# A planner that lets a freed place rest, and one step's transposed weights put ahead of a later step's scores

## The chip, the cores and the metric

One core of one Trainium2 chip. The time is that of one execution in device microseconds. Before the change three runs gave 855.59, 857.68 and 860.67 us; the median, 857.68 us, is what a run of the changed kernel is set against. TensorE is PE below (its weight loads PEld), VectorE is DVE, ScalarE is ACT, GpSimd is POOL, and SP is the queue that issues every load and store.

## The reference, cut to what matters

Three layers in float32. The first is attention that keeps the 32 largest scores of each row; the second mixes four experts; the third is a gated product.

```python
# batch 2, heads 8, 576 positions, head size 64
scores = q @ k.T / 8
kth    = 32nd largest of each row
attn   = softmax(where(scores >= kth, scores, -1e9)) @ v      # -> x, 1152 x 512
p      = domain_probs / sum(domain_probs)                     # 1152 x 4
x      = sum over e of p[:, e] * (relu(x @ w1[e]) @ w2[e])    # w1 512 x 1024, w2 1024 x 512
out    = ((x @ w_a) * (x @ w_b)) @ w_out                      # d_ff 1536
```

## The kernel before, in words

The 1152 tokens lie in nine tiles of 128; the tiles form groups of 1, 2, 3 and 3 (`GROUPS`). Attention goes in 36 steps, counted from n = 0: for each group, for each of four pairs of heads, for each tile of the group. The first group has one tile, so its four pairs are the first to the fourth step (n = 0 to 3). The text counts steps from one: the fourth step is n = 3, the sixth is n = 5.

A step does, for each of its two heads j: `scores` (eight matmuls of 288 columns for the two heads, and ACT's copy of the result at L613 into a place of `ss`); `masked`, which finds the 32 largest on DVE by four MAX8 (L633) and three MATCH_REPLACE8 (L641) for each head; the exponentials and the mask; and `weigh`, which transposes the weights on PE ("turns" them, five transposes a head at L371), copies the result on ACT (L738, L742) into a place of `pts`, and multiplies by v (20 matmuls that read `low` and `vrem`). After a pair's last tile the result is copied to x; for the first group that is L770, into `xf`. The fourth step (`URGENT = 3`) ends the first group, and so has a shorter form of the mask (`hurried`, L698 on ACT, L704 to L709 on DVE).

The first group's experts (`plain`) can finish their first layer only with all four pairs of `xf`: the matmuls `ps<-xf,raw` add up over the pairs, one eight of matmul records for each; L958 then makes the relu on ACT, and the second layer follows (`ps<-raw,low`). Expert weights come by SP into four places of `raw`, and every fifth into `ys`. The later groups' experts are `experts`, with matmuls in three parts (high by high, high by low, low by high) whose results ACT (L870) and DVE (L874, L892) take out of PSUM. The last layer is `gated`.

PSUM has eight banks, held as three kinds of places: `ms` (three single banks, for the experts), `atts` (two pairs of banks, for scores and for every transposed operand of attention) and `os_` (one bank, for weights by v). Places in SBUF belong to a region; `ss` has four, `pts` three.

The order of all instructions is worked out ahead by `Plan.order()`, which walks a calendar with estimated durations. Whenever an engine is free at a point of the calendar, it takes the ready operation with the smallest key whose places are free. Instructions are then issued on each engine in that fixed order; the chip waits by semaphores. An operation that follows another sees its end `SEEN` = 45 ns later, or `SEEN_PE` = 130 ns later where it runs on PE. A place, however, counts as free in the calendar at the instant at which its last user ends.

Places of one kind are handed out in a fixed order as well: each request has a `need`, requests are sorted by it (`settle`), and `place` gives nothing to a request whose turn has not come. For `atts`, `need` equals the operation's key: n - 2.4 for scores (`AHEAD`), n + 0.5 for a step's turned weights, and n - 0.06 for the fourth step's. So the order on the two pairs of banks around the change is: third step's turned weights (2.5, twice), sixth step's scores (2.6, twice), fourth step's turned weights (2.94, twice), then the keys of the next pair of the second batch (3.02, 3.03) and the queries of a later pair (3.04, twice).

Of the kernel before, what the change touches and what calls it, by code (L numbers as in the profile page):

```python
# [34 lines left out]
class Slots:  # L35


    def __init__(self, name, aps, region=None, spans=None):
        self.name, self.aps, self.region, self.spans = name, aps, region, spans
        self.free = set(range(len(aps)))  # L40
        self.queue, self.next = [], 0

    def tile(self, need=0.0):
        t = Buffer(self, need)
        self.queue.append(t)
        return t
# [25 lines left out]
SEEN, SEEN_PE = 45, 130  # L72
# [3 lines left out]
class Plan:  # L76
# [14 lines left out]
    def order(self):  # L91
        for op in self.ops:
            op.left, op.at = len(op.waits), op.since
            for w in op.waits:
                w.after.append(op)
        late, ready, free, events, tick = {}, {}, {}, [], 0
        for op in self.ops:
            for table, empty in ((late, []), (ready, [])):
                table.setdefault(op.engine, list(empty))
            free.setdefault(op.engine, 0.0)  # L100
        for op in self.ops:
            if not op.left:
                heapq.heappush(late[op.engine], (op.at, op.n, op))
        regions = {}
        for s in {id(t.slots): t.slots for op in self.ops for t in op.tiles}.values():
            s.settle()
        for op in self.ops:
            for t in op.tiles:
                s = t.slots
                if s.region is not None and s not in regions.setdefault(s.region, []):  # L110
                    regions[s.region].append(s)
        dma_free, lanes = 0.0, []
        queue, now, done = [(op.since, -1, None) for op in self.ops if op.since], 0.0, []
        heapq.heapify(queue)
        seq = 0

        def place(t):
            s = t.slots
            if t.slot is not None:
                return t.slot  # L120
            if t.n != s.next:
                return None
            for i in sorted(s.free):
                if s.spans is None:
                    return i
                a0, a1 = s.spans[i]
                for o in regions[s.region]:
                    if o is s or o.done:
                        continue
                    if any(a0 < b1 and b0 < a1 for b0, b1 in o.spans):  # L130
                        if o.rank < s.rank or any(
                            j not in o.free and a0 < o.spans[j][1] and o.spans[j][0] < a1 for j in range(len(o.aps))
                        ):
                            break
                else:
                    return i
            return None

        def pick(engine):
            late_, ready_ = late[engine], ready[engine]  # L140
            while late_ and late_[0][0] <= now:
                _, _, op = heapq.heappop(late_)
                heapq.heappush(ready_, (op.key, op.n, op))
            skipped, found = [], None
            stuck = set()
            while ready_:
                item = heapq.heappop(ready_)
                op = item[2]

                ok = not (op.port and free.get("POOL", 0.0) > now)  # L150
                for t in op.tiles:
                    if t.slot is None and (t.slots in stuck or place(t) is None):
                        stuck.add(t.slots)
                        ok = False
                if ok:
                    found = op
                    break
                skipped.append(item)
                if len(skipped) > 60:
                    break  # L160
            for item in skipped:
                heapq.heappush(ready_, item)
            return found

        while len(done) < len(self.ops):
            moved = False
            for engine in free:
                if free[engine] > now:
                    continue
                if engine == "SP" and len(lanes) >= LANES and lanes[-LANES] > now:  # L170
                    continue
                op = pick(engine)
                if op is None:
                    continue
                moved = True
                for t in op.tiles:
                    if t.slot is None:
                        t.slot = place(t)
                        t.slots.free.discard(t.slot)
                        t.slots.next += 1  # L180
                op.start = now
                done.append(op)
                if engine == "SP":
                    free[engine] = now + ISSUE
                    dma_free = max(dma_free, now + ISSUE) + op.nbytes / GBS
                    end = dma_free + LAND
                    lanes.append(end)
                else:
                    free[engine] = now + op.hold
                    end = now + op.hold + op.lag  # L190
                heapq.heappush(queue, (end, op.n, op))
                heapq.heappush(queue, (free[engine], -1, None))
            if moved:
                continue
            if not queue:
                raise RuntimeError("the plan stands still: " + str([(o.n, o.engine, o.key) for o in self.ops if o.start is None][:8]))
            now = max(now, queue[0][0])
            while queue and queue[0][0] <= now:
                _, _, op = heapq.heappop(queue)
                if op is None:  # L200
                    continue
                for t in op.tiles:
                    t.users -= 1
                    if not t.users:
                        t.slots.free.add(t.slot)
                for a in op.after:
                    a.left -= 1
                    a.at = max(a.at, now + (SEEN_PE if a.engine == "PE" else SEEN))
                    if not a.left:
                        heapq.heappush(late[a.engine], (a.at, a.n, a))  # L210
                        heapq.heappush(queue, (a.at, -1, None))
        self.span = now
        return sorted(self.ops, key=lambda o: (o.start, o.n))
# [27 lines left out]
URGENT = 3  # L241


def body(tc, q, k, v, probs, w1, w2, wa, wb, wo, out):
# [109 lines left out]
    def scalar(n, emit, key, after, tiles, sbuf=False, ptr=False, extra=0):  # L354
        return plan.add("ACT", act(n, sbuf, ptr) + extra, emit, key, after, tiles, lag=110)
# [8 lines left out]
    def tensor(hold, emit, key, after, tiles):  # L364
        return plan.add("PE", hold, emit, key, after, tiles, lag=165)
# [4 lines left out]
    def tr(out, a, i):  # L370
        nc.tensor.transpose(out, a, i)  # L371
# [344 lines left out]
    def weigh(pair, i, ed, n):  # L716

        t, T = pair.tiles[i], pair.T
# [3 lines left out]
        pt, ptd = [], []  # L722
        for e, done in ed:

            kt = n + (-0.06 if n == URGENT else 0.5)
            at, p = atts.tile(kt), pts.tile(n)

            def turn(e=e, at=at):
                a = at.ap.rearrange("p b (m c) -> p (b m) c", c=128)
                for m in range(M4):  # L730
                    tr(a[:, m], e.ap[:, m * 128:(m + 1) * 128], ident)
                tr(a[0:REM, M4], e.ap[:, MAIN:S], ident)

            o = tensor(4 * TURN_F + 80, turn, kt, [done, ready], [at, e])

            def ev0(at=at, p=p):
                a = at.ap.rearrange("p b (m c) -> p (b m) c", c=128)
                nc.scalar.activation(p.ap[:, 0:MAIN].rearrange("p (m c) -> p m c", c=128), a[:, 0:M4], AF.Copy)  # L738

            def ev1(at=at, p=p):  # L740
                a = at.ap.rearrange("p b (m c) -> p (b m) c", c=128)
                nc.scalar.activation(p.ap[0:REM, MAIN:MAIN + 128], a[0:REM, M4], AF.Copy)  # L742

            ke = -3000 if n == URGENT else -900
            ptd.append(scalar(512, ev0, ke, [o], [at, p]))
            ptd.append(scalar(128, ev1, ke, [o], [at, p]))
            pt.append(p)
# [367 lines left out]
```

## Time and profile before

| | |
|---|---|
| runs | 855.59, 857.68, 860.67 us; median 857.68 |
| profiled execution | 854.94 us |
| its span | 853.2 us, 14162 instructions |
| busy: PE, PEld, DVE, ACT, POOL | 818.9, 726.6, 717.9, 539.5, 265.4 us |
| mean granted PE clock | 0.989 of full |

The profile is that of one execution. Its page gives each engine's busy time; a second view gives the same for any stretch of the span, with the granted clock (1.00 is 2.4 GHz, 0.50 is 1.2 GHz) and the mean busy share of the 16 DMA engines. A list by time gives each engine's instructions with the idle time before them and, behind an arrow, what ended it. The list of waits adds such idle times up. Matmul ends are modelled, so a run of matmuls is best timed from its first start to the start of what follows.

### The profile page before, as it was taken

What the parts mean: (1) busy time and instruction counts of PE and PEld (TensorE: products, weight loads), DVE (VectorE), ACT (ScalarE), POOL (GpSimd) and SP (SyncE); (2) the same over time, 40 slices, a digit from 0 to 9 for tenths busy, and PEclk for the clock granted to TensorE, in tenths of its full rate; (3) what the DMA queues carried; (4) which work ended last, traced back from release to release, by engine and by line L of the source; (5) the groups of instructions that cost most, each with busy time, mean ns of one, the idle gap of its engine ahead of it and who ended that gap; (6) DMA issues with size and microseconds to landing.
All of it is one profiled execution on the core that took longest, in us unless ns stands there. A gap on an engine that the chain in (4) does not pass through costs nothing.

```text
span 853.2 us, 14162 instructions
## 1 busy us (share of the span) xinstructions
PE 818.9 (96%) x5168; PEld 726.6 (85%) x5168; DVE 717.9 (84%) x1387; ACT 539.5 (63%) x1034; POOL 265.4 (31%) x250
## 2 busy tenths in 40 slices
PE   6689999999999999999999999999999999999997
PEld 5467777789888989888888788899899989999996
DVE  7999999999999999999969999555435888989723
ACT  6878887979989799887656654333225535344210
POOL 4524443897897965863110000000000000000000
PEclk9699999999999999999999999999999999999999
DMA  5939977754564535232345555333001322323003
GB/s 177 284 113 273 334 229 239 222 171 160 171 206 137 176 122 178 77 123 75 99 124 170 188 186 173 123 124 124 1 1 50 99 72 77 99 80 95 25 1 111
DMA packets 83509, 117.06 MB, mean 137 GB/s; under 512 B 10608, under 2 KB 54640, under 8 KB 83440
## 3 DMA queue, kind: packets, MB, share of 16 engines
q1 hardware_dynamic: 83440, 116.17, 43.5%
q8 instruction: 40, 0.66, 0.3%
q14 instruction: 29, 0.24, 0.1%
HBM read 109.07 MB, written 7.08 MB: 136 GB/s over the span
## 4 chain that ended last, share of the span: by engine, by line
PE 73%; DVE 15%; ACT 5%; issue 3%; POOL 2%; DMA 1%; DVEq 0%; POOLq 0%; ACTq 0%
PE ps L368 68%; PE ps L371 5%; DVE low L633 4%; DVE low L641 4%; DVE mid L800 2%; DVE mid L874 1%; ACT mid L799 1%; ACT low L664 1%; POOL low L668 1%; DVE ys L892 1%; DMA raw<-in_moe_w_dram 1%; POOL big L428 1%; ACT low L613 1%; ACT low L683 1%; ACT low L672 0%
## 5 line engine op out<-in xcount | busy, mean ns | idle before, releaser
L368 PE MATMUL ps<-xs,mid 128*128 128x384 f32 (+1 forms) x1152 | 205.9, 322 | 4.0 <-DVE mid L874 3.0
L633 DVE MAX8 low<-low 128x8 f32<-128x576 f32 x288 | 203.8, 746 | 2.2 <-ACT low L613 2.0
L368 PE MATMUL ps<-mid 128*128 128x512 f32 x768 | 197.1, 396 | 1.6 <-DVE mid L874 1.2
L368 PEld LDWEIGHTS ps<-xs,mid 128*128 128x128 f32 x1152 | 183.9, 188 | 14.7 <-DVE mid L874 4.4
L368 PEld LDWEIGHTS ps<-mid 128*128 128x128 f32 x768 | 139.6, 188 | 30.7 <-DVE mid L874 7.2
L641 DVE MATCH_REPLACE8 low<-low 128x576 f32<-128x576 f32 x216 | 159.2, 742 | 0.0
L368 PE MATMUL ps<-xs,big 128*128 128x384 f32 x864 | 152.8, 335 | 0.0
L368 PEld LDWEIGHTS ps<-xs,big 128*128 128x128 f32 x864 | 149.9, 188 | 1.6 <-DVE low L1066 0.3
L799 ACT ACTIVATE mid<-raw 128x1024 fp32r<-128x1024 f32 x96 | 101.3, 1063 | 76.9 <-PE ps L368 36.7
L800 POOL TENSOR_TENSOR mid<-raw,mid 128x1024 fp32r<-128x1024 f32 x48 | 114.9, 2405 | 4.9 <-ACT mid L799 4.5
L668 POOL TENSOR_TENSOR low<-low 128x576 f32<-128x576 f32 x70 | 98.9, 1427 | 38.8 <-ACT low L664 36.1
L368 PE MATMUL ps<-big,mid 128*128 128x512 f32 x324 | 75.0, 390 | 0.0
L800 DVE TENSOR_TENSOR mid<-raw,mid 128x1024 fp32r<-128x1024 f32 x48 | 59.3, 1236 | 17.1 <-ACT mid L799 17.0
L368 PEld LDWEIGHTS ps<-big,mid 128*128 128x128 f32 x324 | 60.7, 188 | 12.3
L892 DVE SCALAR_TENSOR_TENSOR ys<-ps,pr,ys 128x512 f32<-128x512 f32 x56 | 41.5, 746 | 24.8 <-PE ps L368 24.3
L874 DVE SCALAR_TENSOR_TENSOR mid<-ps,mid 128x384 fp32r<-128x384 f32 (+1 forms) x96 | 48.0, 505 | 13.7 <-ACT mid L870 13.6
L683 ACT ACTIVATE low<-low 128x576 f32<-128x576 f32 x70 | 51.4, 776 | 11.4 <-DVE low L680 11.3
L1045 ACT ACTIVATE low<-ps 128x384 f32<-128x384 f32 x36 | 17.6, 490 | 64.0 <-PE ps L368 64.0
L870 ACT ACTIVATE mid<-ps 128x384 fp32r<-128x384 f32 (+1 forms) x96 | 43.1, 452 | 22.0 <-PE ps L368 15.1
L664 ACT ACTIVATE low<-low 128x576 f32<-128x576 f32 x70 | 52.8, 778 | 4.3 <-POOL low L658 4.2
L672 ACT ACTIVATE low<-low 128x576 f32<-128x576 f32 x70 | 54.5, 779 | 0.7 <-POOL low L668 0.7
L613 ACT ACTIVATE low<-ps 128x576 f32<-128x576 f32 x72 | 46.5, 650 | 12.5 <-PE ps L368 6.6
(87 smaller groups left out, 1042.9 us busy)
## 6 DMA issues: line engine op xcount, KB each, us to landing
raw<-in_moe_w_dram SPq DMA_DIRECT2D x122, 512.0 KB, 3.8
big<-kscr SPq DMA_DIRECT2D x20, 576.0 KB, 5.1
low<-in_v_dram SPq DMA_DIRECT2D x24, 256.0 KB, 3.7
low<-in_moe_w_a_dram SPq DMA_DIRECT2D x12, 512.0 KB, 3.8
low<-in_moe_w_b_dram SPq DMA_DIRECT2D x12, 512.0 KB, 3.8
low<-in_moe_w_out_dram SPq DMA_DIRECT2D x12, 512.0 KB, 3.6
kscr<-big SPq DMA_DIRECT2D x8, 576.0 KB, 5.3
ys<-in_moe_w_dram SPq DMA_DIRECT2D x6, 512.0 KB, 5.8
```

The costliest lines, as they stand in the source:

```text
L368: nc.tensor.matmul(out, l, r, **kw)
L613: S, lambda: nc.scalar.activation(s.ap.rearrange("p (c n) -> p c n", c=2), at.ap[:, :, 0:HALF], AF.Copy),
L633: 62 + 1.04 * width, lambda at=at, cs=cs: nc.vector.max(m8v()[:, x, cs], at()), key + 0.02 * r, [done],
L641: lambda at=at, cs=cs: nc.vector.match_replace(out=src[1](), in_to_replace=m8v()[:, x, cs], in_values=at(), imm_value=LOW),
L664: S, lambda x=x, s=s: nc.scalar.activation(e[x].ap, s.ap, AF.Relu, bias=endv()[:, x, 1:2], scale=-STEEP),
L668: pool_(S), lambda x=x, s=s: nc.gpsimd.tensor_tensor(e[x].ap, s.ap, e[x].ap, op=ALU.subtract), ks, [a], [s, e[x]]
L672: lambda x=x: nc.scalar.activation(e[x].ap, e[x].ap, AF.Exp, bias=endv()[:, x, 0:1], scale=scale, accum_out=sums.ap[:, x:x + 1]),
L683: S, lambda x=x: nc.scalar.activation(e[x].ap, e[x].ap, AF.Copy, scale=sums.ap[:, x:x + 1]),
L799: hi = scalar(1024, lambda: nc.scalar.activation(u.ap[:, 0:1024], r.ap, AF.Copy), 500 + s, [ld], [u, r], sbuf=True)
L800: sub = lambda eng: eng.tensor_tensor(u.ap[:, 1024:2048], r.ap, u.ap[:, 0:1024], op=ALU.subtract)
L874: lambda h=h, p=p: nc.vector.scalar_tensor_tensor(h.ap[:, n:2 * n], p.ap[:, 0:n], 0.0, h.ap[:, 0:n], op0=ALU.max, op1=ALU.subtract),
L892: emit = lambda yv=yv, p=p, i=i, e=e: nc.vector.scalar_tensor_tensor(yv(), p.ap, pr[:, i, e:e + 1], yv(), op0=ALU.mult, op1=ALU.add)
```

## The change

Each kind of places gets a `rest`: 130 ns for banks of PSUM, 45 ns for places in SBUF. When the last user of a place ends in the calendar, the place goes back to the free ones only after its rest; until then the planner hands it to nobody. Apart from that the calendar, its durations and its keys are as before. Second, the key of the fourth step's turned weights, and with it their turn at the pairs of banks, goes from 2.94 to 2.55, which is ahead of the sixth step's scores (2.6) and behind the third step's turned weights (2.5). No instruction is added or taken away.

```diff
@@ class Slots
         self.free = set(range(len(aps)))
         self.queue, self.next = [], 0
+
+        self.rest = SEEN_PE if region is None else SEEN
 
@@ Plan.order
                 _, _, op = heapq.heappop(queue)
                 if op is None:
                     continue
+                if isinstance(op, Buffer):
+                    op.slots.free.add(op.slot)
+                    continue
                 for t in op.tiles:
                     t.users -= 1
                     if not t.users:
-                        t.slots.free.add(t.slot)
+                        heapq.heappush(queue, (now + t.slots.rest, -2 - op.n - 0.1 * op.tiles.index(t), t))
@@ weigh
-            kt = n + (-0.06 if n == URGENT else 0.5)
+            kt = n + (-0.45 if n == URGENT else 0.5)
             at, p = atts.tile(kt), pts.tile(n)
```

## Rows read from the trace of the kernel before

**Rows 1.** The page's busy times: engine, us, share of the span, instructions.
```profile
PE 818.9 (96%) x5168; PEld 726.6 (85%) x5168; DVE 717.9 (84%) x1387; ACT 539.5 (63%) x1034; POOL 265.4 (31%) x250
```

**Rows 2.** Busy by stretch: length; PE, PEld, DVE, ACT, POOL; clock, DMA share, GB/s.
```profile
48.00:62.00 14.00, 11.34 (x104) 10.25 (x103) 13.69 (x35) 10.58 (x24) 2.86 (x4) 0.88 0.43 127
62.00:100.00 38.00, 36.52 (x271) 28.94 (x272) 37.13 (x80) 31.89 (x65) 17.76 (x22) 1.00 0.95 300
100.00:300.00 200.00, 197.70 (x1501) 170.09 (x1500) 197.70 (x428) 176.80 (x355) 151.66 (x120) 1.00 0.62 195
300.00:500.00 200.00, 194.84 (x1313) 172.83 (x1312) 189.08 (x357) 150.00 (x289) 69.51 (x65) 1.00 0.41 130
500.00:848.00 348.00, 347.56 (x1805) 319.98 (x1805) 236.47 (x399) 132.90 (x224) 0.00 (x0) 1.00 0.26 81
```

**Rows 3.** PE's waits from 62 to 500 us: total us, times, longest.
```profile
PE ps L368 <- DVE mid L874: 4.2, 7, 1.7
PE ps L368 <- ACT low L958: 1.2, 2, 0.7
PE ps L371 <- ACT low L613: 1.2, 2, 0.6
PE ps L368 <- DMA raw<-in_moe_w_dram: 0.9, 1, 0.9
PE ps L368 <- DVE xs L916: 0.7, 1, 0.7
PE ps L371 <- DVE xs L916: 0.5, 1, 0.5
PE ps L368 <- DVE ys L892: 0.3, 1, 0.3
PE ps L371 <- ACT low L683: 0.3, 1, 0.3
```

**Rows 4.** PE by time: start, us, what, [idle before it <- releaser].
```profile
50.07 2.40 PE L371 MATMUL ps<-identr,low 128*128 128x128 f32 x10 [1.98 <-ACT low L683]
52.12 1.69 PE L368 MATMUL ps<-big 128*128 128x288 f32 x8
53.73 1.09 PE L368 MATMUL ps<-low 128*64 128x128 f32 x16
...
54.98 1.31 PE L371 MATMUL ps<-identr,low 128*128 128x128 f32 x10
56.12 1.06 PE L368 MATMUL ps<-xf,raw 128*128 128x128 f32 x8
...
58.22 1.09 PE L368 MATMUL ps<-low 128*64 128x128 f32 x16
...
60.18 1.12 PE L368 MATMUL ps<-xf,raw 128*128 128x128 f32 x8
62.00 1.12 PE L368 MATMUL ps<-raw,low 128*128 128x512 f32 x2 [0.69 <-ACT low L958]
```

**Rows 5.** DVE by time, the same columns.
```profile
50.35 0.52 DVE L709 TENSOR_SCALAR low<-low 128x576 f32<-128x576 f32 x1
...
52.03 0.52 DVE L709 TENSOR_SCALAR low<-low 128x576 f32<-128x576 f32 x1
...
60.79 2.73 DVE L633 MAX8 low<-low 128x8 f32<-128x576 f32 x4
```

**Rows 6.** ACT by time.
```profile
51.72 0.26 ACT L742 ACTIVATE low<-ps 64x128 f32<-64x128 f32 x1
...
52.78 0.26 ACT L742 ACTIVATE low<-ps 64x128 f32<-64x128 f32 x1
...
61.35 0.60 ACT L958 ACTIVATE low<-ps 128x512 f32<-128x512 f32 x1
```

**Rows 7.** SP's queue by time.
```profile
61.31 1.04 SPq L350 DMA_DIRECT2D raw<-in_moe_w_dram  x2
```

**Rows 8.** One stretch, columns as in rows 2.
```profile
49.50:53.00 3.50, 2.93 (x14) 2.86 (x15) 3.29 (x11) 2.65 (x6) 0.00 (x0) 0.51 0.19 37
```

**Rows 9.** DVE by time around the longest of PE's waits.
```profile
489.66 1.22 DVE L800 TENSOR_TENSOR mid<-raw,mid 128x1024 fp32r<-128x1024 f32 x1
490.80 0.55 DVE L874 SCALAR_TENSOR_TENSOR mid<-ps,mid 128x384 fp32r<-128x384 f32 x1
```

**Rows 10.** PE by time, what that wait held up.
```profile
491.40 0.80 PE L368 MATMUL ps<-xs,mid 128*128 128x384 f32 x3 [1.65 <-DVE mid L874]
```

## The prediction

> **What bounds the kernel now.** I read the page's busy times first, then busy time by stretch, then PE's waits, and last the lists by time around 48 to 62 us, where the moved transposes stand. The reader is to see in the first that PE is busy 96% of the span and no other engine over 85% [rows 1]. The second shows where the rest lies: from 62 to 848 us PE is busy in 776.62 of 786 us, so only 9.4 us of idle time are left in nine tenths of the span, 1.5, 2.3, 5.2 and 0.4 us in the four stretches [rows 2]. From 100 to 300 us DVE is just as full (197.70 of 200), so there two engines run at their limit together; from 500 us on PE alone does. No PE work is added or removed by this change. The end can therefore come earlier only by what PE's idle time shrinks, and later by what it grows, apart from the clock.
>
> The waits say what that idle time is: 9.3 us in eight kinds and 15 places, of which 4.2 us wait for L874, where DVE takes an expert's result out of a bank, 1.2 us for the relu L958, 1.2 us for the copy L613 and 0.9 us for one weight load [rows 3]. One relu wait, 0.69 us, stands exactly at 62.00 us [rows 4] and belongs to the place of the change.
>
> **Part one: the turned weights of the fourth step.** In the list by time PE does the third step's turns at 50.07, the sixth step's scores at 52.12, weights by v of the third step at 53.73, the fourth step's turns at 54.98, its weights by v at 58.22, the last eight of the first layer at 60.18, and then nothing until the relu lets the second layer start at 62.00 [rows 4].
>
> The new order puts ten transposes where eight score matmuls were. When can they run? The first head's mask ends at 50.35 + 0.52 = 50.87, the second's at 52.03 + 0.52 = 52.55 [rows 5]. The pairs of banks come free when the third step's copies end, at 51.72 + 0.26 = 51.98 and 52.78 + 0.26 = 53.04 [rows 6]. So the first head turns at 52.12, right behind the third step's turns; five transposes at the half clock, which holds until about 53 us [rows 8], take half of 52.12 - 50.07, 1.0 us. The second head turns from 53.1 on, and at full clock takes half of 56.12 - 54.98, 0.6 us. PE idles about 0.15 us between them. The third step's weights by v then start at 53.7, as before: the transposes cost there what the scores cost (1.61 us from 52.12 to 53.73).
>
> The second head's copy needs a place of `pts`. There are three, two hold the third step's weights, and one of these comes free at about 55.0, when that product ends. With 0.75 us of copying the fourth step's product can start at 55.9 instead of 58.22, 2.3 us sooner. What follows it follows at the same distances, so the second layer could start at 59.7.
>
> What of that reaches the end? Only idle time. Between 53 and 62 us PE has the same work in either order: the displaced scores, two rounds of key and query transposes and one eight of the first layer remain as filler, together more than 3 us, for the gaps of the faster chain. So I count the 0.69 us before 62.00 as gone and the 0.15 us as new. The 0.9 us wait for a weight load [rows 3] is behind that. The two loads that SP issues at 61.31 go out when the last eight of the first layer give up their places [rows 7], so about 2.3 us sooner. The DMA engines are 43% busy before 62 us and 95% after it [rows 2]: work moved into the emptier stretch shortens the backlog behind it, but the places for later loads come free only as fast as PE works, and PE is then 0.5 us ahead, not 2.3. I take half of the 0.9, 0.45 us; the ends are nothing and all of it. Sum of part one: -0.69 + 0.15 - 0.45 = -1.0 us.
>
> Covers: the scores of the sixth step are needed when DVE opens that step. The four MAX8 from 60.79 are the last two of the fifth step and the first two of the sixth [rows 5], so it opens near 62.1. The scores now wait for the turns' copies, the second head's until about 55.9; with matmuls and copy they are there by 57.3, almost 5 us early. If that cover were gone, each late microsecond would be DVE's, which has no reserve. PE's queue gains a wait: the turns now stand where they must wait for a mask and for a copy, and all of PE stands behind them; that is the 0.15 us. On SP the two weight loads pass a load of v and one of k; they hold the queue for 1.04 us [rows 7], and keys are prepared more than a step ahead of use, so I count nothing. POOL has no part in the hurried form after its bias product.
>
> **Part two: the rest.** It changes only where the calendar places things, so its price is a new deal of PE's waits. How true is it? In the trace DVE's L874 ends at 490.80 + 0.55 = 491.35 and PE starts on it at 491.40 [rows 9, 10]; L958 ends at 61.95 and PE starts at 62.00 [rows 4, 6]. PE follows in 0.05 us. The calendar said nothing for a bank, and will say 0.130. For PE the error changes sign and doesn't shrink. For SBUF's 45 ns it does shrink.
>
> How much can the order move? Each kind of place is given out in a fixed sequence, and every attention operand takes a pair of banks; so attention's own order on PE stays, and so does that of the experts. Only how the two are interleaved can move, and the queues of ACT and DVE that empty their banks. At most 15 x 0.13 = 2 us of the waits are of the kind that a rest of 130 ns could have foreseen. From both sides: all waits after 62 us other than the two above could go, 9.3 - 0.7 - 0.9 = 7.7 us, or as many could be added. The nearest rows, those of L874, don't speak for either: the longest, 1.65 us, arose because L874 stood behind a 1.22 us subtraction at L800 on DVE [rows 9, 10], which a rest does not see. I take zero and keep both ends.
>
> The sum, against the profiled execution's 854.94 us, is 853.9 us. That execution lies 2.7 us under the median of the runs, so on the runs' scale it is 857.68 - 1.0 = 856.7 us.
>
> **The rivals.** *The waits go.* A calendar that is truer for DVE's and ACT's places sends fewer instructions ahead of a bank that still holds a result. All 7.7 us gone give 849.0 us; with the 1.0 us of part one it becomes visible once 3.3 us of them go. For it: 15 places, mean 0.6 us, most behind one kind of reader. Against it: the row of L800, and the 130 ns that overshoot.
>
> *DVE takes banks out later.* This is the slower side. PE's expert matmuls have three banks, and DVE empties them in line with its own work. Where the new interleaving puts one more instruction ahead of an L874, the bank comes back 0.75 to 1.2 us later, PE finds none free, and the time is lost since PE has no reserve afterwards. Seven such waits cost 4.2 us now [rows 3]; if the waits of 62 to 500 us double, 7.7 us are added, and 857.68 - 1.0 + 7.7 = 864.4 us. It decides from 5.3 us added, nine more waits. For it: DVE at 197.70 of 200 us, ACT at 176.80. Against it: the fixed sequences, and the unchanged keys that put L874 ahead of the search for the largest.
>
> *The clock stays low.* The granted clock is 0.51 from 49.5 to 53 us, after PE had stood idle for 1.98 us [rows 4, 8]; it is at 1.2 GHz while PE does the third step's turns. With ten more transposes in place of matmuls the rise could come a stretch later: 3.4 us more at half, 1.7 us lost, 858.4 us. Against it: PE's work there is as dense as before.
>
> *PE was not the limit.* The Trainium skill, "Trainium Kernel Development and Optimization", section Performance Expectations, says that matmul busy time is a bad metric because matmuls are pipelined, and that the busy share of weight loads is a good one. On that reading PE has room. By the rows PE's weight loads fill 170.09 of 200 us from 100 to 300 us while DVE fills 197.70; if DVE alone sets the pace there, a gain on PE is absorbed and the time stays 857.7 us. But from 500 to 848 us the weight loads fill 319.98 of 348 us where PE waits for nothing, so part of the 15% is only the pace of wide matmuls [rows 2]; I give it little.
>
> **How the numbers follow.** Forecast 0.53, with 853.5 to 860 us as its own range (3 us of new deal either way); clock 0.06; DVE as the limit 0.06; waits gone 0.21; banks late 0.14. A measurement of this kernel can tell about 0.5%, 4.3 us, from no change; the first three cases lie within it, so 0.65 for the same, 0.21 faster, 0.14 slower. The range for 8 in 10 reaches to 849.5 and to 862.5 us, most of the way into both outer cases.
>
> **What would show it.** The fourth step's ten transposes start near 52.1 and 53.1, its product near 56, the second layer near 59.7, without 0.69 us of idle time before it. PE's idle time from 62 to 848 us is 8 to 9 us, and DVE opens the sixth step without a wait. The prediction is wrong if PE's waits after 100 us go under 4 us or over 13 us, if DVE waits for L613 near 62 us, or if the low clock lasts past 54 us.

## The result, and the profile after

Four runs of the changed kernel gave 849.56, 848.04, 850.36 and 849.24 us, median 849.4; four of the kernel before had a median of 857.66 us. The ratio is 0.9900, 95% interval 0.9867 to 0.9932. The change is faster, by 8.3 us of the medians; the forecast was 856.7 us, no change that can be measured, and the range ended 0.1 us above the time. The profiled execution of the changed kernel has a span of 847.8 us.

The change adds five lines ahead of all that is named here, so L874 of before is L879, L870 is L875, L799 is L804, L800 is L805, L371 is L376 and L368 is L373.

First the busy times by stretch after, columns as in [rows 2]:

```profile
48.00:62.00 14.00, 12.30 (x113) 10.38 (x114) 13.69 (x35) 11.34 (x25) 2.93 (x4) 1.00 0.49 144
62.00:100.00 38.00, 37.23 (x280) 29.46 (x279) 38.00 (x84) 31.89 (x66) 17.86 (x22) 1.00 0.94 306
100.00:300.00 200.00, 197.29 (x1494) 169.27 (x1494) 197.01 (x427) 179.39 (x363) 149.85 (x120) 0.99 0.61 191
300.00:500.00 200.00, 197.84 (x1327) 177.30 (x1326) 191.65 (x366) 149.77 (x284) 73.66 (x64) 1.00 0.43 136
```

PE's idle time falls by 1.0 us around the moved transposes (48 to 62 us), by 0.7 us to 100 us, and by 3.0 us between 300 and 500 us, where it was 5.2 us [rows 2]; from 100 to 300 us it grows by 0.4 us. The waits from 62 to 500 us after, against [rows 3]:

```profile
PE ps L376 <- DVE mid L879: 2.1, 3, 1.0
PE ps L373 <- DVE mid L879: 1.3, 1, 1.3
PE ps L376 <- ACT low L688: 0.9, 3, 0.4
PE ps L376 <- ACT low L618: 0.4, 1, 0.4
PE ps L373 <- ACT low L963: 0.3, 1, 0.3
PE ps L373 <- POOL mid L805: 0.3, 1, 0.3
PE ps L376 <- DVE xs L921: 0.2, 1, 0.2
```

5.5 us instead of 9.3 us. The wait for a weight load is gone. Now the list by time that answers to [rows 4]:

```profile
50.35 2.11 PE L376 MATMUL ps<-identr,low 128*128 128x128 f32 x15 [1.15 <-ACT low L688]
52.39 1.09 PE L373 MATMUL ps<-low 128*64 128x128 f32 x16
...
53.63 0.77 PE L376 MATMUL ps<-identr,low 128*128 128x128 f32 x5
54.15 0.78 PE L373 MATMUL ps<-big 128*128 128x288 f32 x4
...
56.76 1.09 PE L373 MATMUL ps<-low 128*64 128x128 f32 x16
...
59.01 1.12 PE L373 MATMUL ps<-xf,raw 128*128 128x128 f32 x8
...
60.94 1.12 PE L373 MATMUL ps<-raw,low 128*128 128x512 f32 x2 [0.52 <-ACT low L963]
```

The first head of the fourth step turns with the third step's two (x15; the eleventh starts at 51.69), the second at 53.63, its product starts at 56.76 and the second layer at 60.94: 1.06 us sooner than before, with 0.52 us of the wait for the relu left. The order alone did not do that: the granted clock is 1.00 from 49.5 to 53 us here and was 0.51 before [rows 8], and the third step's ten turns took 1.34 us instead of 2.05.

To see where the rest comes from I set the two traces against each other by work done: every matmul start counts with the median distance to the next start of its kind, and the lead is how much sooner the changed kernel has done the same sum. The lead is 1.05 us at 62 us, -0.5 us at 420 us, 3.7 us at 500 us and 5.3 us at 640 us, and it stays there (the spans differ by 5.4 us). The early lead is lost between 100 and 200 us, where PE waits 1.32 us for L879 until 163.07 and the clock stands at 0.50 from 164 to 167 us. So the change's large part arises after 420 us, in the stage where attention ends and the experts of the last groups run, and in part where PE's row shows no idle time. What happens there is seen in the kernel before, once in each period of 16.9 us; by time, start, us, what, [idle before it <- releaser]:

```profile
546.55 0.69 PE L368 MATMUL ps<-xs,mid 128*128 128x384 f32 x3
...
547.14 1.06 ACT L799 ACTIVATE mid<-raw 128x1024 fp32r<-128x1024 f32 x1 [1.07 <-PE ps L368]
548.11 0.47 ACT L870 ACTIVATE mid<-ps 128x384 fp32r<-128x384 f32 x1
548.24 1.23 DVE L800 TENSOR_TENSOR mid<-raw,mid 128x1024 fp32r<-128x1024 f32 x1 [1.58 <-ACT mid L799]
549.38 0.55 DVE L874 SCALAR_TENSOR_TENSOR mid<-ps,mid 128x384 fp32r<-128x384 f32 x1
549.98 1.00 PEld L368 LDWEIGHTS ps<-mid 128*128 128x128 f32 x5 [0.41 <-DVE mid L874]
```

The three matmuls from 546.55 end a group: with them the place of split weights `w` comes free, and the result that the relu L870 takes out is complete. ACT has been waiting for just that, and then starts L799, the split of the *next* weights into the freed place, 1.06 us long; the relu follows a microsecond late. On DVE the second half of the split, L800, stands ahead of L874 in the same way. PE's weight load waits for L874. After the change, the same spot:

```profile
543.57 0.49 ACT L875 ACTIVATE mid<-ps 128x384 fp32r<-128x384 f32 x1 [2.48 <-PE ps L373]
543.96 1.05 ACT L804 ACTIVATE mid<-raw 128x1024 fp32r<-128x1024 f32 x1
544.09 0.56 DVE L879 SCALAR_TENSOR_TENSOR mid<-ps,mid 128x384 fp32r<-128x384 f32 x1 [1.90 <-ACT mid L875]
545.04 1.23 DVE L805 TENSOR_TENSOR mid<-raw,mid 128x1024 fp32r<-128x1024 f32 x1 [0.39 <-ACT mid L804]
```

The relu and L879 go first, and nothing on PE waits. Before the change the weight loads from 500 to 640 us waited for L874 in seven places; after it the list has no such wait:

```profile
PEld ps L368 <- DVE mid L874: 2.8, 7, 0.5
```

The calendar's arithmetic says why. The relu has key -1000 and would always win against the split (500 and more). But the calendar let the split see the free place at the instant of the matmuls' end, and the relu see their result 45 ns later: for 45 ns ACT had only the split to take. With a rest of 45 ns both are seen at once, and the key decides. The same exists on PE: the DVE instruction that frees a bank of `m` also makes the operand of a group further ahead in the order; the bank was seen at once, the operand 130 ns later, and PE took a later group first.

### The profile page after: what moved, and what is told of

Same layout as the page of the kernel before. It is cut to its first block, busy times and chain, and to the rows that moved or that the text cites. A ratio compares the mean times of both kernels' runs of the same rounds, so it can differ in the third digit from the quotient of the medians.

```text
span 847.8 us, 14175 instructions
## 1 busy us (share of the span) xinstructions
PE 817.2 (96%) x5168; PEld 728.4 (86%) x5168; DVE 715.7 (84%) x1387; ACT 537.5 (63%) x1034; POOL 267.5 (32%) x250
## 4 chain that ended last, share of the span: by engine, by line
PE 78%; DVE 10%; ACT 7%; issue 2%; POOL 1%; DMA 0%; POOLq 0%; ACTq 0%; DVEq 0%
PE ps L373 72%; PE ps L376 6%; DVE low L638 3%; DVE low L646 2%; DVE mid L805 1%; ACT low L688 1%; ACT low L618 1%; ACT low L669 1%; ACT big L429 1%; ACT low L677 1%; ACT big L570 1%; DVE mid L879 1%; ACT low L743 1%; POOL big L433 1%; POOL low L673 1%
## 5 line engine op out<-in xcount | busy, mean ns | idle before, releaser
L373 PE MATMUL ps<-xs,mid 128*128 128x384 f32 (+1 forms) x1152 | 204.1, 322 | 1.3 <-DVE mid L879 1.3
L373 PE MATMUL ps<-mid 128*128 128x512 f32 x768 | 198.3, 395 | 0.3 <-POOL mid L805 0.3
L373 PEld LDWEIGHTS ps<-xs,mid 128*128 128x128 f32 x1152 | 186.0, 191 | 9.6 <-DVE mid L879 1.5
L373 PEld LDWEIGHTS ps<-mid 128*128 128x128 f32 x768 | 139.5, 188 | 24.0 <-DVE mid L879 0.7
L373 PE MATMUL ps<-xs,big 128*128 128x384 f32 x864 | 152.6, 335 | 0.0
L373 PEld LDWEIGHTS ps<-xs,big 128*128 128x128 f32 x864 | 150.2, 188 | 1.2 <-DVE xs L921 0.2
L804 ACT ACTIVATE mid<-raw 128x1024 fp32r<-128x1024 f32 x96 | 101.5, 1061 | 43.4 <-issue 27.2
L805 POOL TENSOR_TENSOR mid<-raw,mid 128x1024 fp32r<-128x1024 f32 x48 | 115.3, 2407 | 15.3 <-ACT mid L804 11.3
L875 ACT ACTIVATE mid<-ps 128x384 fp32r<-128x384 f32 (+1 forms) x96 | 43.6, 455 | 51.4 <-PE ps L373 46.0
L373 PE MATMUL ps<-big,mid 128*128 128x512 f32 x324 | 76.0, 391 | 0.0
L373 PEld LDWEIGHTS ps<-big,mid 128*128 128x128 f32 x324 | 60.5, 188 | 12.5 <-DVE low L1053 0.4
L879 DVE SCALAR_TENSOR_TENSOR mid<-ps,mid 128x384 fp32r<-128x384 f32 (+1 forms) x96 | 48.4, 507 | 26.0 <-ACT mid L875 25.5
L805 DVE TENSOR_TENSOR mid<-raw,mid 128x1024 fp32r<-128x1024 f32 x48 | 58.5, 1220 | 9.6 <-ACT mid L804 8.8
L688 ACT ACTIVATE low<-low 128x576 f32<-128x576 f32 x70 | 51.4, 778 | 12.4 <-DVE low L685 12.4
L669 ACT ACTIVATE low<-low 128x576 f32<-128x576 f32 x70 | 51.9, 778 | 9.8 <-POOL low L663 9.7
L376 PE MATMUL ps<-identr,low 128*128 128x128 f32 (+1 forms) x360 | 50.0, 279 | 5.2 <-ACT low L688 4.6
```

Source lines behind the costliest of these rows:

```text
L373: nc.tensor.matmul(out, l, r, **kw)
L669: S, lambda x=x, s=s: nc.scalar.activation(e[x].ap, s.ap, AF.Relu, bias=endv()[:, x, 1:2], scale=-STEEP),
L688: S, lambda x=x: nc.scalar.activation(e[x].ap, e[x].ap, AF.Copy, scale=sums.ap[:, x:x + 1]),
L804: hi = scalar(1024, lambda: nc.scalar.activation(u.ap[:, 0:1024], r.ap, AF.Copy), 500 + s, [ld], [u, r], sbuf=True)
L805: sub = lambda eng: eng.tensor_tensor(u.ap[:, 1024:2048], r.ap, u.ap[:, 0:1024], op=ALU.subtract)
L875: n, lambda h=h, p=p: nc.scalar.activation(h.ap[:, 0:n], p.ap[:, 0:n], AF.Relu), -1000, [o], [h, p]
```

## The experiments

The first theory was that of the weights' places (`w`); its rivals were that the earlier start of part one is carried to the end, that any new order deals PE's waits anew, and that a calendar nearer to the chip is what helps. The table has the ratio to the kernel before on the same chip, and two readings of the profile: PE's idle time from 420 to 500 us, and the time that weight loads wait for L874 (L879) from 500 to 640 us. The kernel before had medians of 857.65 us beside key_only, rest_only, all_w44 and w_rest, 856.09 us beside late400, mw_rest_key, seen0 and before_again, and 857.57 us beside the last four, so runs are compared by their ratios. The edits shown are against the changed kernel.

| run | median us | ratio, 95% interval | PE idle 420-500 | weight loads' wait |
|---|---|---|---|---|
| before | 857.66 | 1 | 3.8 | 2.8 |
| after | 849.4 | 0.9900 (0.9867 to 0.9932) | 1.0 | none |
| key_only | 854.08 | 0.9963 (0.9951 to 0.9976) | 3.8 | 2.8 |
| rest_only | 851.18 | 0.9916 (0.9901 to 0.9930) | 1.9 | none |
| all_w44 | 853.21 | 0.9947 (0.9933 to 0.9961) | 2.8 | 2.6 |
| w_rest | 856.21 | 0.9981 (0.9970 to 0.9992) | 2.1 | 3.9 |
| late400 | 849.64 | 0.9929 (0.9909 to 0.9950) | 1.2 | none |
| mw_rest_key | 853.95 | 0.9963 (0.9947 to 0.9979) | 1.9 | none |
| seen0 | 854.45 | 0.9979 (0.9967 to 0.9991) | 1.1 | none |
| before_again | 857.49 | 1.0010 (0.9992 to 1.0027) | 3.8 | 2.8 |
| late400_key | 848.40 | 0.9892 (0.9874 to 0.9911) | 1.3 | none |
| mw_late_key | 847.83 | 0.9882 (0.9861 to 0.9902) | 1.0 | none |
| early400 | 858.07 | 1.0000 (0.9986 to 1.0015) | 3.8 | 3.0 |
| all_m129 | 851.11 | 0.9919 (0.9903 to 0.9934) | 1.0 | 1.1 |

**The two parts alone.**

```diff
 # key_only
-        self.rest = SEEN_PE if region is None else SEEN
+        self.rest = 0
 # rest_only
-            kt = n + (-0.45 if n == URGENT else 0.5)
+            kt = n + (-0.06 if n == URGENT else 0.5)
```

> Only the fourth step's key is changed (2.55); no place rests. The whole change gave 8.3 us. By the first theory (a resting place of the expert weights keeps ACT's weight split L799 behind the relu's copy L870 late in the kernel; part one gives about 1 us) the time is about 1 us under before, 856 to 857.5 us, and PE still waits 6 to 8 us after 420 us. By its rival (the earlier start of the first group's second layer is carried to the end) it has most of the gain, 850 to 852 us.

> Only the rest; the fourth step's key stays 2.94. By the first theory the time is 849.5 to 852 us, with PE's waits from 420 to 640 us cut as in the changed kernel. By the rival (the earlier start) it is within 2 us of before, 856 to 859 us. By a second rival (any new order deals PE's waits anew, with no one cause) it can come out anywhere from 848 to 862 us.

The rest has most of the gain, with the late waits cut; the early start alone does not carry it. But the key gives 0.37%, 3.2 us, three times what either text expected; the late waits in its profile are those of before, so its gain is made early.

**One nanosecond.**

```diff
 # all_w44                         (w_rest: SEEN if name == "w" else 0, key -0.06)
-        self.rest = SEEN_PE if region is None else SEEN
+        self.rest = 44 if name == "w" else SEEN_PE if region is None else SEEN
 # all_m129
+        self.rest = 129 if name == "m" else SEEN_PE if region is None else SEEN
```

> The changed kernel, but the places of split expert weights (w) rest 44 ns and not 45; all else is the same. 45 ns is when the relu's copy sees the same matmul end, so with 44 the split is again the first to be free on ACT, by 1 ns. By the first theory about 5 us of the gain are gone, 853 to 856 us, nearly all of it lost after 420 us. By the rival that a calendar nearer to the chip is what helps, one nanosecond can change nothing: 849 to 850.5 us.

> Only the places of split expert weights (w) rest, 45 ns; no other place rests and the fourth step's key stays 2.94. By the first theory this alone carries the late gain: 851.5 to 854 us, PE's waits on L874 after 420 us mostly gone. If the rest of PSUM banks is needed (second theory: PE sends its experts' matmuls too soon at banks that look free), it stays at 856 to 859 us.

> The changed kernel, but the experts' three banks (m) rest 129 ns and not 130, so that PE sees a bank 1 ns before the DVE result that ended with it. 44 instead of 45 for the weights' places gave back 4 us of the gain. Theory of the two jumps: the second half of the late gain goes, 851 to 854 us, with weight loads waiting for DVE from 500 to 640 us. Rival (only the weights' places matter, or a truer calendar): 849 to 850.5 us.

With 44 instead of 45 ns the ratio goes from 0.9900 to 0.9947, and the weight loads' waits are back: no truer calendar explains a step within one nanosecond, the order of two sightings does. `w` alone, however, missed its expectation: PE's idle time from 420 to 500 us falls from 3.8 to 2.1 us, but from 500 to 640 us more is lost than before. These are the waits of the weight loads in that stretch, of w_rest, all_w44 and all_m129, in that order:

```profile
PEld ps L373 <- DVE mid L879: 3.9, 9, 0.5
```
```profile
PEld ps L373 <- DVE mid L879: 2.6, 6, 0.5
```
```profile
PEld ps L373 <- DVE mid L879: 1.1, 4, 0.3
```

With `m` at 129 ns there are four again where the changed kernel has none; its time, 0.9919, can't be told from the changed kernel's, but by work done its lead grows by 0.3 us from 500 to 640 us, where the changed kernel's grows by 1.6 us. So the theory was half of it, and `m` was added.

Both jumps can be counted in the calendars, which need no chip. After 400 us a split is taken 45 ns before a relu of smaller key is seen 19 times in the kernel before, 20 times in key_only and 18 times in early400; in all_w44 it is 18 times by 1 ns, and in the other kernels there is none. PE takes a group of the second layer 130 ns before one of smaller key is seen seven times in the kernel before and in key_only and five times in early400, in all_m129 five times by 1 ns, and in the other kernels never. In w_rest this second jump is missing too: PE takes a group up to 116 ns too soon there twelve times (nine in the kernel before, two in the changed one), behind other pairs of instructions. So what a rest of `m` removes is wider than the tie of one instruction, and which pairs cost w_rest its time is not shown.

**Only late, and only two kinds.**

```diff
 # late400 (key -0.06), late400_key (key -0.45); early400: now < 400e3, key -0.45
-   heapq.heappush(queue, (now + t.slots.rest, ...
+   heapq.heappush(queue, (now + (t.slots.rest if now > 400e3 else 0), ...
 # mw_rest_key, and mw_late_key with the line above
+        self.rest = SEEN if name == "w" else SEEN_PE if name == "m" else 0
```

> The rest holds only where the calendar is past 400 us; before that, and in the fourth step's key, the plan is that of the kernel before. By the first theory the late gain (5 us of PE's idle time after 420 us) is there in full and nothing else is: 852 to 854 us, PE idle 1 to 2 us from 420 to 520 us instead of 3.9, no weight load waiting for the banks' DVE pass from 500 to 640 us. By the rival that the early order is carried to the end, 856.5 to 859 us.

> The new key, and a rest for two kinds of places alone: split expert weights (w, 45 ns) and the three banks of the experts (m, 130 ns). The run with w alone gained from 420 to 500 us and lost it again from 500 to 640 us. If the two kinds of jump (ACT's split ahead of the relu's copy, PE's next group ahead of the one whose DVE result ended with the bank) are the whole late cause, 849.5 to 852 us and no weight load waits for the banks' DVE pass from 500 to 640 us. If the rest of all kinds is needed, or any new order deals the waits anew, 853 to 857 us.

> The new key, and the rest of all kinds only where the calendar is past 400 us. The key alone gave a ratio of 0.9963 and the late rest alone 0.9929. If the two gains lie in separate stages (key: the weight load that PE waits for near 75 us; rest: the banks after 420 us) they add: 0.989 to 0.991, about 847.5 to 849 us, at or below the changed kernel's 849.4. If the early gain is swallowed by the stage from 62 to 420 us, the ratio stays at 0.993, 851.5 us.

> As the run before in this list, but after 400 us only two kinds of places rest: split expert weights (w) and the experts' three banks (m). The run with m and w over the whole calendar had PE's late waits gone but lost 3.3 us near 285 us, at one wait for a weight split on POOL that its new order made. Theory of the two jumps: with the order up to 400 us kept, the same time as the run with all kinds, 847.5 to 849.5 us. Rival (all kinds must rest late): 852 us or more.

> The new key, and the rest of all kinds only up to 400 us of the calendar. By the theory PE's late waits are back, 3 to 4 us idle from 420 to 520 us and weight loads waiting for the banks' DVE pass from 500 to 640 us; the key's gain stays, so 853 to 856 us. By the rival that the early order is carried to the end, 849 to 851 us, as the changed kernel.

The late rest alone gives 0.9929, 851.6 us on the scale of 857.66 and a little better than expected. Times the key's 0.9963 that is 0.9892, which is what both together measured: the two gains lie in separate stages and add. With two kinds of places the late waits go as with all (mw_late_key, 0.9882): `w` and `m` suffice. Over the whole calendar the same two kinds gave only 0.9963, and 853.95 us lies in the range of the rivals; no weight load waits for L879 late there either, but by work done 3.6 us are lost from 200 to 300 us, around a wait near 285 us which of the other traces only that of seen0 has (elsewhere it is 0.3 us or not there). PE's waits from 270 to 300 us in mw_rest_key, and then in seen0:

```profile
PE ps L373 <- POOL mid L805: 2.2, 1, 2.2
```
```profile
PE ps L373 <- POOL mid L805: 2.9, 1, 2.9
```

There a split on POOL comes late, and the granted clock falls around it: 0.76 from 284 to 288 us and 0.81 to 292 us in mw_rest_key, 0.68 and 0.50 in seen0. early400 missed its expectation: the late waits are back as foreseen, but the key's gain does not show. By work done it is 0.5 us ahead of key_only at 420 us and 2.1 us behind the first trace of before at 500 us; its late order is not that of before but a new one with the ties unresolved. How much of the loss is that order's is not shown, for the clock falls there too (0.96 from 420 to 500 us). Beside the late rest the early rest is worth about nothing: the changed kernel's ratio, 0.9900, lies on that of late400_key, 0.9892. What it is worth by itself stays open.

**A tie without any rest.**

```diff
-SEEN, SEEN_PE = 45, 130
+SEEN, SEEN_PE = 0, 0
```

> The new key, but nothing rests, and the calendar's other delay is gone too: an operation sees what it follows at the instant of its end (0 and 0 ns instead of 45 and 130). Places and results are then seen at one instant, as with the rest, and the smaller key wins; but the calendar is further from the chip than either kernel's. By the theory that the tie is what matters: 849 to 852 us, with the late waits gone. By the rival that a truer calendar matters: 855 us or more, with PE's late waits as before or longer.

The total missed and comes near the rival's 855 us; its trace loses 7.5 us by work done from 200 to 300 us, around the wait at 286 us above. In the stage in question it did what the theory said: 1.1 us idle from 420 to 500 us and no weight load that waits for L879, with a calendar further from the chip than before.

**The kernel before, once more.**

> The kernel before, unchanged, for a second profile and time. The first profile was of a fast execution (854.94 us, median 857.65). By both theories about 857.7 us; the profile shows whether the slower executions differ by a stretch of low granted clock after PE's idle time at 488 to 491 us, or by something else.

Its span is 858.6 us, 5.4 us over the first. Three places make it. By 62 us it is 2.1 us behind by work done; the granted clock from 42 to 62 us is 0.74 here and 0.91 in the first trace. Next, PE's wait for a weight load, 0.9 us in the first trace [rows 3], is 2.3 us here, and DVE stands in line behind it. PE by time, and DVE's wait from 62 to 100 us:

```profile
77.99 1.16 PE L368 MATMUL ps<-xf,raw 128*128 128x128 f32 x8 [2.26 <-DMA raw<-in_moe_w_dram]
```
```profile
DVE ys L972 <- PE ps L368: 2.2, 1, 2.2
```

In key_only, whose granted clock up to 62 us was the same (0.69 from 20 to 42 us and 0.74 from 42 to 62 us in both), scores and second-layer matmuls stand at this place of PE's order, and it waits for nothing:

```profile
74.67 1.02 PE L373 MATMUL ps<-raw,low 128*128 128x512 f32 x2
75.58 0.80 PE L373 MATMUL ps<-big 128*128 128x288 f32 x4
76.22 1.02 PE L373 MATMUL ps<-raw,low 128*128 128x512 f32 x2
77.17 1.09 PE L373 MATMUL ps<-low 128*64 128x128 f32 x16
```

By work done both are 2.1 us behind the first trace at 62 us, so with the same clock the key gains nothing up to there (the second layer starts at 64.12 in before_again and at 64.06 us in key_only); at 420 us before_again is 3.6 us behind and key_only level. The key's load does not go out sooner either: the one that PE waits for is issued at 70.46 us in before_again and at 70.43 us in key_only, but the eight matmuls that read it start at 77.99 and at 82.44 us. Third, after the waits of 0.48 and 1.66 us for L916 and L874, the clock falls; busy times by stretch:

```profile
492.00:496.00 4.00, 2.00 (x12) 1.62 (x13) 4.00 (x8) 2.23 (x5) 0.00 (x0) 1.00 0.55 151
496.00:500.00 4.00, 4.00 (x16) 4.00 (x16) 3.65 (x7) 0.63 (x1) 0.00 (x0) 0.57 0.80 241
```

That costs another 1.5 us by work done. The first trace has the same waits [rows 10] and no such fall; key_only has both.

## Why the prediction was wrong, point by point

**What bounds the kernel** held: the gain is PE's idle time that went, 9.4 us between 62 and 848 us at most. (The rows count 16 waits, not 15; nothing hangs on it.) It was short in one respect: PE's busy row does not show all of it. From 500 to 640 us, before and after, columns as in [rows 2]:

```profile
500.00:640.00 140.00, 139.57 (x709) 125.44 (x709) 82.33 (x117) 51.05 (x75) 0.00 (x0) 1.00 0.32 99
500.00:640.00 140.00, 139.61 (x724) 128.31 (x723) 78.86 (x109) 49.94 (x75) 0.00 (x0) 1.00 0.30 94
```

PE is equally busy in both, yet the lead grows by 1.6 us there; the waits of the weight loads show the difference. The rule of the Trainium skill, "Trainium Kernel Development and Optimization", section Performance Expectations, which the prediction set aside with a small chance, calls the busy share of the weight loads a good measure. The trace agrees: that share tells the two apart, 125.44 against 128.31 us of 140. The use that the prediction made of the rule (PE has room, so the gain is absorbed) did not come true.

**Part one, -1.0 us,** had the right sign, a mis-sized term and the wrong reason for it. The transposes, the product and the second layer came at 51.69 and 53.63, 56.76 and 60.94 us, against 52.1 and 53.1, 55.9 and 59.7; the product waits on PE behind scores and transposes that the fixed order puts there, and 0.52 us of the relu's wait remained. With equal clocks the second layer starts not 2.3 us sooner but 1.17 us (62.11 in rest_only and 60.94 in the changed kernel, both at 1.00 from 42 to 62 us) or 0.06 us (before_again and key_only). The term that failed is the weight load: "I take half of the 0.9, 0.45 us". All of it goes, and in before_again it was 2.3 us and stopped DVE for 2.2 us. It goes because PE's new order puts the matmuls that read the load later, and not because the load is issued sooner. Other waits go with it: PE's idle time from 62 to 300 us is 3.8, 5.9 and 4.1 us in before, before_again and late400, and 2.0, 2.2 and 1.9 us in key_only, late400_key and mw_late_key. Measured alone, the part is worth 3.2 us (2.1 to 4.2); whether another new order of that stage would give as much is not shown. The prediction's sum stood on one execution 2.7 us under the median, and the load's wait differs between executions of the same early order: 0.9 us in before, 2.3 us in before_again, none in late400.

**Part two, zero,** is the step that decided. It was "I take zero and keep both ends", with two reasons that both failed. The first was that the longest wait "arose because L874 stood behind a 1.22 us subtraction at L800 on DVE [rows 9, 10], which a rest does not see": the rest is what puts L800 behind L874. The second was "At most 15 x 0.13 = 2 us of the waits are of the kind that a rest of 130 ns could have foreseen": the 45 and 130 ns are not the price; they decide which of two instructions goes first, and the price is up to the length of the wrong one, 1.06 us on ACT and 1.23 us on DVE. The late rest alone measured 0.9929, 6.1 us (4.3 to 7.8). The sentence "Only how the two are interleaved can move, and the queues of ACT and DVE that empty their banks" named the place, and gave it no price.

**The rivals.** The waits went, as the first rival had it, at 849.0 us against 849.4 measured. That the two agree is luck: of its 7.7 us of waits 5.5 us are left from 62 to 500 us, and the rest of the gain lay in waits of weight loads that it did not count and in the early order. Its reason, a truer calendar, fell with all_w44 and seen0. Banks taken out later did not happen in this order, but it exists: in w_rest weight loads wait 3.9 us for L879 from 500 to 640 us, against 2.8 us before. The clock did not stay low in the profiled execution: it is 1.00 from 48 to 62 us. In key_only it is 0.50 from 52.5 to 55.5 us, past the 54 us that were to show this rival, but so it is in before_again without the change.

## What to carry to other kernels

In a list scheduler, a freed place and the result of the instruction that frees it must become visible at the same instant; otherwise the operation that needs only the place can jump the one with priority, and a delay of 45 ns can cost up to the length of a whole instruction. Read the order of two instructions that one event releases: where the long one without urgency goes first, look for such a tie. When an estimate stands on one execution, ask which of its waits and clocks another would have differently. With the key and the late rest for two kinds of places alone the kernel ran at 847.83 us, 0.9882 (0.9861 to 0.9902): under both kernels' medians, though not apart from the changed kernel by its interval.

## What the runs showed of the hardware

The granted clock can fall late in a kernel that is 96% busy: after two waits of PE of together 2.1 us it stood at 0.57 from 496 to 500 us in one execution of the kernel before, and not in another with the same waits. In the changed kernel it stood at 0.50 from 164 to 167 us, after a wait of 1.32 us.
